# Transpositions woven between products, in a fused attention and FFN kernel

## The chip, the cores and the metric

The kernel runs on one core of a Trainium2 chip. The metric is the device time of one execution in microseconds (us); a profiled execution has a span from its first to its last instruction. Engines are named as in the profile: PE is TensorE's matrix products and PEld its weight loads, DVE is VectorE, ACT is ScalarE, POOL is GpSimd, SP is SyncE, which issues most transfers.

## The reference

Hashed attention over 4 batches of 8 heads (768 rows of 64), then a gated FFN over all 3072 tokens:

```
q_bits, k_bits = (q @ proj > 0), (k @ proj > 0)          # 6 bits: a bucket for each row
mask = q_bucket[:, None] == k_bucket[None, :]
scores = where(mask, (q @ k.T) / sqrt(64), -1e9)
attn = softmax(scores);  x = concat_heads(attn @ v)      # 3072 x 512
h = x @ w_in;  g = h * clip(h + 3, 0, 6) / 6;  out = g @ w_out   # 512 -> 2048 -> 512
```

## The kernel before

Work goes in 192 **steps** k, one for 128 query rows of a head (six steps a head, KT = 6). What one step does to the rows of its own number, and in which step it is emitted:

- `scores` (L305, L308; S below): four products of 384 columns into a PSUM pair `s`, emitted three steps ahead: step k emits S(k+3).
- `lowest` (L315): VectorE reads `s`, takes the row minimum and writes the tile `p`; step k emits `lowest(k+2)`. There are two `p` tiles, so p(k+2) takes the place of p(k).
- `exponential` (L327): ScalarE, in place on `p`; step k emits that of k+1.
- `transp` (L337; T below): six transpositions of 128 x 128 turn p(k) into two PSUM tiles `pt` (halves c = 0 and 1, three each).
- `split_p` (L360, L361): for each half ScalarE writes the high part `ph` and VectorE the rest `pl`.
- `values` (L374, L375; V below): for two steps' rows together, six products of 256 columns for each half, ph and pl in turn with v, into the PSUM tile `acc`. A half of the pair (k-2, k-1) is done in step k, the other in step k+1 (k even); from k = 102 on both in step k.
- `output` (L402): ScalarE copies `acc` to `y`.

Every sixth step holds a **hash** of the next head (`hash_qk`, L265 to L267: six products z, and `bits`, L276, on VectorE). The FFN of a chunk of 256 tokens is, for each of 16 slices, `gemm1` (L478 to L480, twelve products of 256 columns into `h`), `gate` on ScalarE and VectorE, and `gemm2` (L500 to L502, six products of 512 columns into `po`). The FFN of the first batch runs between steps 49 and 53; that of the others fills the steps from about 98 on, a `gemm1` and a `gemm2` of the slice before in each. `normalise` (rt, L436) transposes the softmax's divisors for it.

The order on TensorE, VectorE, ScalarE and GpSimd is that in which the program is written; every engine works through its own queue in order. `bank` hands out four PSUM banks in turn to pt, acc and h; `pair` hands out two bank pairs to s and z while no FFN runs (they alternate), and one alone once `ffn_on` is set. So while the FFN fills the steps, S(k+3) must wait until `lowest(k+2)` has read the pair.

In a step the main loop emits, before the change: T(k); `exponential(k+1)`; `lowest(k+2)`; V; the FFN's `gemm1`; S(k+3) (with the hash ahead of it); `split_p(k)`; `gemm2`.

Of the kernel before, what the change touches and what calls it, by code (L numbers as in the profile page):

```python
# [18 lines left out]
P = 128  # L19
NB = 6  # L20
ZK = 96
ZM = ZK + 2 * NB
# [18 lines left out]
def lsh_attention_moe(  # L41
# [10 lines left out]
    nc = tc.nc  # L52
# [3 lines left out]
    KT = S // P  # L56
    HW = S // 2
    QT = HW // P
    NCC = DM // P
    NFC = DF // P  # L60
# [3 lines left out]
    KM = D + 2 * NB  # L64
# [14 lines left out]
    def bank(shape, name: str, tag: str | None = None):  # L79

        nonlocal turn
        if tag is None:
            tag = ("pt", "pu")[turn % 2]
            turn += 1
        return ps.tile(shape, F32, name=name, tag=tag, bufs=2)
# [4 lines left out]
    def pair(name: str):  # L90

        nonlocal pair_turn
        pair_turn += 1
        tag = "s" if ffn_on or pair_turn % 2 else "po"
        return ps.tile([P, 2, 512], F32, name=name, tag=tag, bufs=1)


    thr = cp.tile([P, 1], F32, name="thr")
# [2 lines left out]
    ident = cp.tile([P, P], F32, name="ident")  # L101
# [3 lines left out]
    pjl = cp.tile([P, ZM], F32R, name="pjl")  # L105
# [3 lines left out]
    pjk, pjq = pjh[:, :ZM], pjh[:, ZK - D :]  # L109
# [97 lines left out]
    GB = HK + FB  # L207
# [22 lines left out]
    def scale_q(i: int):  # L230

        nc.gpsimd.tensor_scalar_mul(raws[i][:D], raws[i][:D], -SCALE)
# [27 lines left out]
    def hash_qk(i: int):  # L260
        k1, k2, q1, q2 = state[i]
        z = zs[i] = pair(f"z{i}")
        for j in range(2):
            c = slice(j * HW, (j + 1) * HW)
            nc.tensor.matmul(z[:ZM, j, :HW], lhsT=pjl[:], rhs=q1[:, c], start=True, stop=False)  # L265
            nc.tensor.matmul(z[:ZM, j, :HW], lhsT=pjk, rhs=k2[:, c], start=False, stop=False)
            nc.tensor.matmul(z[:ZM, j, :HW], lhsT=pjq, rhs=q2[:, c], start=False, stop=True)  # L267

    def bits(i: int):
        k1, k2, q1, q2 = state[i]  # L270
# [25 lines left out]
    scs, probs, outs = {}, {}, {}  # L296

    def scores(g: int):
        i, t = divmod(g, KT)
        k1, k2, q1, q2 = state[i]  # L300
        us = slice(t * P, (t + 1) * P)
        s = scs[g] = pair(f"s{g}")
        for c in range(2):
            cs_ = slice(c * HW, (c + 1) * HW)
            nc.tensor.matmul(s[:, c, :HW], lhsT=q1[:KM, us], rhs=k1[:KM, cs_], start=True, stop=False)  # L305
        for c in range(2):
            cs_ = slice(c * HW, (c + 1) * HW)
            nc.tensor.matmul(s[:, c, :HW], lhsT=q2[:, us], rhs=k2[:, cs_], start=False, stop=True)  # L308

    def lowest(g: int):  # L310

# [19 lines left out]
    pts, parts = {}, {}  # L331
    halves = 0

    def transp(g: int, c: int):
        pt = pts[g, c] = bank([P, QT, P], f"pt{g}_{c}")
        for x in range(QT):
            nc.tensor.transpose(pt[:, x], probs[g][0][:, c, x * P : (x + 1) * P], ident[:])  # L337
        if c:
            del probs[g]

    lent = []

# [23 lines left out]
    def values(u: int, c: int):  # L366
        vv = vvs[2 * u // KT]
        if c == 0:
            accs[u] = bank([P, 2 * P], f"acc{u}")
        acc = accs[u]  # L370
        hi, lo = parts.pop((u, c))
        for x in range(QT):
            kt = c * QT + x
            nc.tensor.matmul(acc[:], lhsT=vv[:, kt], rhs=hi[:, x], start=(kt == 0), stop=False)  # L374
            nc.tensor.matmul(acc[:], lhsT=vv[:, kt], rhs=lo[:, x], start=False, stop=(kt == KT - 1))  # L375

    adds = []

# [93 lines left out]
    def gemm1(n: str, fc: int, x, tag: str | None = None):  # L472
        hp = bank([P, TC], f"h{n}_{fc}", tag)
        wi = wt[2 * fc]
        for cc in range(NCC):
            xh, xl = x[cc]
            wc = slice(cc * P, (cc + 1) * P)
            nc.tensor.matmul(hp[:], lhsT=wi[:, 0, wc], rhs=xh, start=(cc == 0), stop=False)  # L478
            nc.tensor.matmul(hp[:], lhsT=wi[:, 0, wc], rhs=xl, start=False, stop=False)  # L479
            nc.tensor.matmul(hp[:], lhsT=wi[:, 1, wc], rhs=xh, start=False, stop=(cc == NCC - 1))  # L480
        return hp

    def gate(n: str, fc: int, hp, copy, engine, between=lambda: None):
# [12 lines left out]
    def gemm2(fc: int, po, gh, gl):  # L496
        wo = wt[2 * fc + 1]
        for u in range(TC // P):
            us = slice(u * P, (u + 1) * P)
            nc.tensor.matmul(po[u], lhsT=gh[:, us], rhs=wo[:, 0], start=(fc == 0), stop=False)  # L500
            nc.tensor.matmul(po[u], lhsT=gh[:, us], rhs=wo[:, 1], start=False, stop=False)  # L501
            nc.tensor.matmul(po[u], lhsT=gl[:, us], rhs=wo[:, 0], start=False, stop=(fc == NFC - 1))  # L502

    def store(b: int, t: int, po, end: bool = False):
        ob = sp.tile([P, TC // P, DM], F32, name=f"ob{b}_{t}", tag="ob")
# [283 lines left out]
    def lead(j: int):  # L789

        i, t = divmod(j, KT)
        n = i + 1
        alone = j < GF + LA
        if t == 0 and n < NJ:
            split_qk(n, nc.scalar.copy if ffn_on else nc.gpsimd.tensor_copy)
        if t in (1, 4):
            add()
        if t == 2:
            if i:
                split_v(i)  # L800

            if n + 1 < NJ and n != H + 1:
                get_qk(n + 1)
        if t == 3 and n < NJ:
            get_v(n)
            if alone:
                hash_qk(n)
        scores(j)
        if t == 3 and n < NJ and alone:
            bits(n)  # L810
        if t == 4 and n + 1 < NJ:
            scale_q(n + 1)
# [27 lines left out]
    with tc.manual_schedule(engines={ET.PE, ET.DVE, ET.Activation, ET.Pool}):  # L840
        split_qk(0, None)
        hash_qk(0)
        bits(0)
        scale_q(1)
        split_v(0)
        for x in range(3):
            ahead(0, x)
        for k in range(NS):
            end = GB if k < GB else NS
            i, t = divmod(k, KT)  # L850
            if k == HK - XE:
                lent += [cp.tile([P, 2 * WC], F32R, name=f"lent{n}", tag="w", bufs=NW) for n in range(2)]
            if k == GB:
                lent.clear()
            if k == HK:
                late["x"] = sp.tile([P, S], F32, name="late", tag="raw", bufs=1)
            for c in range(2):
                transp(k, c)
            if k + 1 < end:
                exponential(k + 1)  # L860
            if k + 2 < end:
                lowest(k + 2)
            if k == GB:
                next(first)
                pair_turn = 0

            third = k < GF + 2
            whole = False
            for _ in range(1 if third and k != HK else (2, 0)[k % 2]):
                if vnext < k - k % 2:  # L870
                    whole = value_half()
            if k >= GF - 2:
                next(fill, None)
            if whole and k >= GF:
                output(vnext // 2 - 1)
                whole = False

            hashed = k >= GF and (k + LA) % KT == 2
            if k >= GF and k + LA < end and not hashed:
                lead(k + LA)  # L880
            for c in range(2):
                split_p(k, c, third)
            if (k < GF or hashed) and k + LA < end:
                if hashed:
                    if (k + LA) // KT + 1 < NJ:
                        hash_qk((k + LA) // KT + 1)
                        bits((k + LA) // KT + 1)
                    next(fill, None)
                lead(k + LA)
            if whole:  # L890
                output(vnext // 2 - 1)
            if k >= GF - 2 and not hashed:
                next(fill, None)
            if k + LA >= NS:
                add()
            if HK - XE <= k < GB:
                for f in early_steps[k - HK + XE]:
                    f()

            if k < HK and t == 1 and i:  # L900
                with tc.issue_after(last.ins):
                    for n in range((i - 1) * WE // (H - 1), i * WE // (H - 1)):
                        load_w(n)
            if k == HK:
                late_x()
                with tc.issue_after(last.ins):
                    get_qk(H + 2)
                    for n in range(WE, WL):
                        load_w(n)
            if k + 1 == GB:  # L910
                first = first_ffn(lambda part: ahead(GB, part))
                next(first)
                for _ in range(2):
                    whole = value_half()
                output(vnext // 2 - 1)
                next(first)
        while vnext < NS:
            if value_half():
                output(vnext // 2 - 1)
        add()  # L920
        for _ in fill:
            pass
# [47 lines left out]
```

## Time and profile before

| | |
|---|---|
| median of 3 runs | 1042.86 us (1040.63 to 1043.05) |
| the profiled execution | 1040.82 us |
| its span | 1039.0 us |
| mean granted TensorE clock | 0.994 |
| PE busy / DVE busy | 97% / 66% of the span |
| L337 transpositions | 1152, 275 ns each as recorded, 162.2 us in all |

How rows read: "start us, us, engine line op out<-in xcount" in the views by time, where a row merges neighbours of one kind and a bracket gives the idle time before it and what ended it; recorded products overlap, so the distance between starts tells what one costs, and its duration does not. Rows of waits read "waiter <- releaser: us in total, times, longest us".

### The profile page before, as it was taken

To read this page: it belongs to the slowest core of one execution; us is meant where nothing else is said; L and a number is where in the kernel's file an instruction comes from. 1 tells how busy PE (TensorE), PEld (TensorE's weight loads), DVE (VectorE), ACT (ScalarE), POOL (GpSimd) and SP (SyncE) were. 2 spreads that over 40 slices of the span, in tenths; PEclk is the share of its full clock that TensorE was granted. 3 is DMA by queue.
4 is the path that set the end of the run, shared out by engine and by line. 5 is a ranking of instruction groups with operands and counts; after the bars stand their busy time and mean duration, and the time that the engine had idled before them with its cause. 6 is when DMAs were issued, how large, how long until landed. Compare 5 with 4: busy or idle time off the path is not lost.

```text
span 1039.0 us, 18911 instructions
## 1 busy us (share of the span) xinstructions
PE 1009.5 (97%) x6846; PEld 927.2 (89%) x6846; DVE 687.0 (66%) x1441; ACT 583.6 (56%) x1308; POOL 451.4 (43%) x439
## 2 busy tenths in 40 slices
PE   8999879999999999999999999999999999999998
PEld 7999868887989998899999999999899999899997
DVE  6999888999479998766656666655665563333332
ACT  6888855555478887645554555454455462333332
POOL 5677753334247775645444444544454232200100
PEclk9999989999999999999999999999999999999999
DMA  3666686000144555322222232222232011101000
GB/s 93 155 149 155 187 277 236 1 2 1 46 130 112 120 124 143 80 53 60 75 46 63 61 88 59 53 71 59 60 93 47 15 37 28 42 1 41 1 22 20
DMA packets 47380, 80.68 MB, mean 78 GB/s; under 512 B 5892, under 2 KB 27780, under 8 KB 47288
## 3 DMA queue, kind: packets, MB, share of 16 engines
q1 hardware_dynamic: 42808, 73.98, 24.2%
q0 software_dynamic: 4480, 5.51, 4.6%
q8 instruction: 54, 0.88, 0.4%
q14 instruction: 38, 0.31, 0.1%
HBM read 41.95 MB, written 18.09 MB: 58 GB/s over the span
## 4 chain that ended last, share of the span: by engine, by line
PE 83%; DVE 8%; issue 3%; POOL 2%; ACT 2%; DMA 1%; SPq 0%; DVEq 0%; POOLq 0%; ACTq 0%
PE pt L337 11%; PE h L479 7%; PE h L478 7%; PE h L480 7%; PE po L500 7%; PE po L502 7%; PE po L501 7%; PE acc L374 6%; PE acc L375 6%; PE s L305 6%; PE s L308 6%; DVE wr L175 1%; DVE pl L361 1%; DVE wr L177 1%; PE z L267 1%
## 5 line engine op out<-in xcount | busy, mean ns | idle before, releaser
L315 DVE TENSOR_SCALAR_CACHE_REDUCE p<-s 128x768 f32<-128x768 f32 x192 | 183.5, 956 | 103.5 <-PE pt L337 99.5
L361 DVE TENSOR_TENSOR pl<-pt,ph 128x384 fp32r<-128x384 f32 x376 | 191.8, 551 | 50.4 <-ACT ph L360 48.3
L360 ACT CAST ph<-pt 128x384 fp32r<-128x384 f32 x376 | 165.5, 480 | 57.4 <-PE pt L337 45.0
L327 ACT ACTIVATE p<-p,m 128x768 f32<-128x768 f32 x192 | 179.5, 935 | 5.1 <-DVE p L315 4.8
L487 ACT ACTIVATE g<-h,three 128x256 f32<-128x256 f32 x192 | 91.4, 476 | 155.9 <-PE h L480 141.6
L337 PE MATMUL pt<-ident,p 128*128 128x128 f32 x1152 | 162.2, 275 | 5.9 <-DVE pl L361 4.8
L493 POOL TENSOR_TENSOR gl<-g,gh 128x256 fp32r<-128x256 f32 x96 | 74.2, 773 | 203.7 <-DVE gh L492 160.0
L488 DVE SCALAR_TENSOR_TENSOR g<-g,h 128x256 f32<-128x256 f32 x192 | 80.6, 420 | 117.8 <-ACT g L487 115.3
L337 PEld LDWEIGHTS pt<-ident,p 128*128 128x128 f32 x1152 | 137.3, 141 | 23.6 <-PE pt L337 3.8
L374 PE MATMUL acc<-ph,vv 128*128 128x256 f32 x564 | 152.8, 303 | 1.0 <-DVE pl L361 1.0
L478 PE MATMUL h<-xh,w 128*128 128x256 f32 x512 | 147.7, 289 | 1.2 <-ACT y L402 1.2
L480 PE MATMUL h<-xh,w 128*128 128x256 f32 x512 | 143.4, 280 | 1.3 <-POOL w L196 1.3
L479 PE MATMUL h<-xl,w 128*128 128x256 f32 x512 | 143.2, 280 | 0.6 <-DVE xl L470 0.6
L375 PE MATMUL acc<-pl,vv 128*128 128x256 f32 x564 | 141.1, 283 | 0.0
L500 PE MATMUL po<-w,gh 128*128 128x512 f32 x320 | 126.7, 396 | 1.5 <-ACT gh L492 1.4
L501 PE MATMUL po<-w,gh 128*128 128x512 f32 x320 | 126.2, 394 | 0.9 <-POOL w L196 0.9
L502 PE MATMUL po<-w,gl 128*128 128x512 f32 x320 | 126.6, 396 | 0.0
L374 PEld LDWEIGHTS acc<-ph,vv 128*128 128x128 f32 x564 | 107.5, 191 | 2.2 <-DVE pl L361 1.9
L375 PEld LDWEIGHTS acc<-pl,vv 128*128 128x128 f32 x564 | 107.9, 191 | 0.0
L305 PE MATMUL s<-kk,qq 76*128 76x384 f32 x384 | 101.2, 344 | 2.5 <-ACT kk L281 1.5
L308 PE MATMUL s<-kk,qq 128*128 128x384 f32 x384 | 100.0, 341 | 0.0
L478 PEld LDWEIGHTS h<-xh,w 128*128 128x128 f32 x512 | 96.4, 188 | 3.8 <-ACT y L402 2.4
(134 smaller groups left out, 1999.5 us busy)
## 6 DMA issues: line engine op xcount, KB each, us to landing
raw<-in_qkT SPq DMA_DIRECT2D x32, 384.0 KB, 3.5
kk<-qq SPq DMA_DIRECT2D x62, 192.0 KB, 3.2
wr<-in_w_in SPq DMA_DIRECT2D x16, 512.0 KB, 7.1
wr<-in_w_out SPq DMA_DIRECT2D x16, 512.0 KB, 3.8
vr<-in_v SPq DMA_DIRECT2D x32, 192.0 KB, 2.4
qq<-qq SPq DMA_DIRECT2D x31, 192.0 KB, 3.6
out<-ob SPq DMA_DIRECT2D x11, 512.0 KB, 3.0
xr<-xs SPq DMA_DIRECT2D x9, 512.0 KB
```

Of the source, the lines that this page charges most:

```text
L315: nc.vector.tensor_scalar(out=pr_[:], in0=s[:, :, :HW], scalar1=CAP, scalar2=None, op0=ALU.min, op1=ALU.min, accum_out=m[:],)
L327: nc.scalar.activation(pr_[:], pr_[:], AF.Exp, bias=m[:], scale=-1.0, accum_out=sms[b][:, t, h : h + 1])
L337: nc.tensor.transpose(pt[:, x], probs[g][0][:, c, x * P : (x + 1) * P], ident[:])
L361: nc.vector.tensor_sub(lo[:, :, w], pt[:], hi[:, :, w].bitcast(F32))
L374: nc.tensor.matmul(acc[:], lhsT=vv[:, kt], rhs=hi[:, x], start=(kt == 0), stop=False)
L375: nc.tensor.matmul(acc[:], lhsT=vv[:, kt], rhs=lo[:, x], start=False, stop=(kt == KT - 1))
L478: nc.tensor.matmul(hp[:], lhsT=wi[:, 0, wc], rhs=xh, start=(cc == 0), stop=False)
L479: nc.tensor.matmul(hp[:], lhsT=wi[:, 0, wc], rhs=xl, start=False, stop=False)
L480: nc.tensor.matmul(hp[:], lhsT=wi[:, 1, wc], rhs=xh, start=False, stop=(cc == NCC - 1))
L500: nc.tensor.matmul(po[u], lhsT=gh[:, us], rhs=wo[:, 0], start=(fc == 0), stop=False)
L501: nc.tensor.matmul(po[u], lhsT=gh[:, us], rhs=wo[:, 1], start=False, stop=False)
L502: nc.tensor.matmul(po[u], lhsT=gl[:, us], rhs=wo[:, 0], start=False, stop=(fc == NFC - 1))
```

## The change

The six transpositions of a step are no longer emitted in one run. `transp` puts them on a list `woven`, and each product that is emitted through the new `mm` is followed by one of them, until the list is empty. Products of V, hash, S and FFN go through `mm`; the normalising transpositions do not. What is left is emitted by `flush` ahead of `split_p`, and in step GB = 52 at once.

```diff
+    woven = []
+
+    def mm(out: bass.AP, **kw):
+        nc.tensor.matmul(out, **kw)
+        if woven:
+            woven.pop(0)()
...
-    def transp(g: int, c: int):
-        pt = pts[g, c] = bank([P, QT, P], f"pt{g}_{c}")
-        for x in range(QT):
-            nc.tensor.transpose(pt[:, x], probs[g][0][:, c, x * P : (x + 1) * P], ident[:])
-        if c:
-            del probs[g]
+    def transp(g: int):
+
+        pr_, _ = probs.pop(g)
+
+        def one(x: int):
+            nc.tensor.transpose(
+                pts[g, x // QT][:, x % QT], pr_[:, x // QT, (x % QT) * P : (x % QT + 1) * P], ident[:]
+            )
+
+        for c in range(2):
+            pts[g, c] = bank([P, QT, P], f"pt{g}_{c}")
+        woven.extend(lambda x=x: one(x) for x in range(KT))
+
+    def flush():
+        while woven:
+            woven.pop(0)()
...
-            nc.tensor.matmul(acc[:], lhsT=vv[:, kt], rhs=hi[:, x], start=(kt == 0), stop=False)
-            nc.tensor.matmul(acc[:], lhsT=vv[:, kt], rhs=lo[:, x], start=False, stop=(kt == KT - 1))
+            mm(acc[:], lhsT=vv[:, kt], rhs=hi[:, x], start=(kt == 0), stop=False)
+            mm(acc[:], lhsT=vv[:, kt], rhs=lo[:, x], start=False, stop=(kt == KT - 1))
...
-            for c in range(2):
-                transp(k, c)
+            transp(k)
+            if k == GB:
+                flush()
...
             if k >= GF and k + LA < end and not hashed:
                 lead(k + LA)
+            flush()
             for c in range(2):
                 split_p(k, c, third)
```

(In `hash_qk`, `scores`, `gemm1` and `gemm2` the products change to `mm` in the same way.)

TensorE in the even step 36, before the change: scores, the run of six, then the six products of V(36), whose first carries the wait on VectorE. In the names, pt36_0 is half 0 of step 36, and ph17_0 and pl17_0 hold half 0 of the pair 34 and 35.

```order
L305 MATMUL s38_1449<-kk_6_1161,qq_6_1162 128x384 x2
L308 MATMUL s38_1449<-kk_6_1161,qq_6_1162 128x384 x2
L337 MATMUL pt36_0_1456<-ident_69,p36_1399 128x128 [waits DVE_49,Activation_49]
L337 MATMUL pt36_0_1456<-ident_69,p36_1399 128x128 x2
L337 MATMUL pt36_1_1460<-ident_69,p36_1399 128x128 [waits Activation_49]
L337 MATMUL pt36_1_1460<-ident_69,p36_1399 128x128 x2
L374 MATMUL acc17_1468<-ph17_0_1408,vv5_1231 128x256 [waits DVE_49,PE_49]
L375 MATMUL acc17_1468<-pl17_0_1409,vv5_1231 128x256
```

The same place after it (L100 is `mm`, L346 the transposition):

```order
L100 MATMUL s38_1449<-kk_6_1161,qq_6_1162 128x384 x4
L100 MATMUL acc17_1462<-ph17_0_1408,vv5_1231 128x256 [waits DVE_49,Activation_49]
L346 MATMUL pt36_0_1456<-ident_69,p36_1393 128x128 [waits DVE_49,PE_49]
L100 MATMUL acc17_1462<-pl17_0_1409,vv5_1231 128x256
L346 MATMUL pt36_0_1456<-ident_69,p36_1393 128x128
L100 MATMUL acc17_1462<-ph17_0_1408,vv5_1231 128x256
L346 MATMUL pt36_0_1456<-ident_69,p36_1393 128x128
L100 MATMUL acc17_1462<-pl17_0_1409,vv5_1231 128x256
L346 MATMUL pt36_1_1457<-ident_69,p36_1393 128x128 [waits Activation_49]
```

V(36) moved directly behind the scores, and the second wait on VectorE, now on the first transposition, is that for pl17_0 of step 35, which the product behind it reads.

TensorE in the odd step 121, in the part with the FFN, before: the run, then the first of twelve `gemm1` products (h1_0_15), behind which S(124) stands.

```order
L337 MATMUL pt121_0_6605<-ident_69,p121_6481 128x128 [waits Activation_49]
L337 MATMUL pt121_0_6605<-ident_69,p121_6481 128x128 x2
L337 MATMUL pt121_1_6609<-ident_69,p121_6481 128x128 [waits DVE_49]
L337 MATMUL pt121_1_6609<-ident_69,p121_6481 128x128 x2
L478 MATMUL h1_0_15_6617<-xh1_0_5665,w30_3392 128x256
```

The same place after it, from the step's first product to its last transposition:

```order
L100 MATMUL h1_0_15_6611<-xh1_0_5665,w30_3392 128x256 [waits Activation_49]
L346 MATMUL pt121_0_6605<-ident_69,p121_6475 128x128 [waits DVE_49,PE_49]
L100 MATMUL h1_0_15_6611<-xl1_0_5666,w30_3392 128x256
L346 MATMUL pt121_0_6605<-ident_69,p121_6475 128x128
L100 MATMUL h1_0_15_6611<-xh1_0_5665,w30_3392 128x256
L346 MATMUL pt121_0_6605<-ident_69,p121_6475 128x128
L100 MATMUL h1_0_15_6611<-xh1_0_5665,w30_3392 128x256
L346 MATMUL pt121_1_6606<-ident_69,p121_6475 128x128 [waits DVE_49]
L100 MATMUL h1_0_15_6611<-xl1_0_5666,w30_3392 128x256
L346 MATMUL pt121_1_6606<-ident_69,p121_6475 128x128
L100 MATMUL h1_0_15_6611<-xh1_0_5665,w30_3392 128x256
L346 MATMUL pt121_1_6606<-ident_69,p121_6475 128x128
```

The last transposition moved behind six of the twelve products; the other six and S(124) still follow it. On VectorE, ScalarE and GpSimd the order is the same before and after.

More of the change, by code (lines that the diff above doesn't have):

```diff
@@ L264, in hash_qk @@
             c = slice(j * HW, (j + 1) * HW)
-            nc.tensor.matmul(z[:ZM, j, :HW], lhsT=pjl[:], rhs=q1[:, c], start=True, stop=False)
-            nc.tensor.matmul(z[:ZM, j, :HW], lhsT=pjk, rhs=k2[:, c], start=False, stop=False)
-            nc.tensor.matmul(z[:ZM, j, :HW], lhsT=pjq, rhs=q2[:, c], start=False, stop=True)
+            mm(z[:ZM, j, :HW], lhsT=pjl[:], rhs=q1[:, c], start=True, stop=False)
+            mm(z[:ZM, j, :HW], lhsT=pjk, rhs=k2[:, c], start=False, stop=False)
+            mm(z[:ZM, j, :HW], lhsT=pjq, rhs=q2[:, c], start=False, stop=True)
     def bits(i: int):
@@ L304, in scores @@
             cs_ = slice(c * HW, (c + 1) * HW)
-            nc.tensor.matmul(s[:, c, :HW], lhsT=q1[:KM, us], rhs=k1[:KM, cs_], start=True, stop=False)
+            mm(s[:, c, :HW], lhsT=q1[:KM, us], rhs=k1[:KM, cs_], start=True, stop=False)
         for c in range(2):
             cs_ = slice(c * HW, (c + 1) * HW)
-            nc.tensor.matmul(s[:, c, :HW], lhsT=q2[:, us], rhs=k2[:, cs_], start=False, stop=True)
+            mm(s[:, c, :HW], lhsT=q2[:, us], rhs=k2[:, cs_], start=False, stop=True)
     def lowest(g: int):
@@ L477, in gemm1 @@
             wc = slice(cc * P, (cc + 1) * P)
-            nc.tensor.matmul(hp[:], lhsT=wi[:, 0, wc], rhs=xh, start=(cc == 0), stop=False)
-            nc.tensor.matmul(hp[:], lhsT=wi[:, 0, wc], rhs=xl, start=False, stop=False)
-            nc.tensor.matmul(hp[:], lhsT=wi[:, 1, wc], rhs=xh, start=False, stop=(cc == NCC - 1))
+            mm(hp[:], lhsT=wi[:, 0, wc], rhs=xh, start=(cc == 0), stop=False)
+            mm(hp[:], lhsT=wi[:, 0, wc], rhs=xl, start=False, stop=False)
+            mm(hp[:], lhsT=wi[:, 1, wc], rhs=xh, start=False, stop=(cc == NCC - 1))
         return hp
@@ L499, in gemm2 @@
             us = slice(u * P, (u + 1) * P)
-            nc.tensor.matmul(po[u], lhsT=gh[:, us], rhs=wo[:, 0], start=(fc == 0), stop=False)
-            nc.tensor.matmul(po[u], lhsT=gh[:, us], rhs=wo[:, 1], start=False, stop=False)
-            nc.tensor.matmul(po[u], lhsT=gl[:, us], rhs=wo[:, 0], start=False, stop=(fc == NFC - 1))
+            mm(po[u], lhsT=gh[:, us], rhs=wo[:, 0], start=(fc == 0), stop=False)
+            mm(po[u], lhsT=gh[:, us], rhs=wo[:, 1], start=False, stop=False)
+            mm(po[u], lhsT=gl[:, us], rhs=wo[:, 0], start=False, stop=(fc == NFC - 1))
     def store(b: int, t: int, po, end: bool = False):
```

## The prediction

> **What bounds the kernel now.** I read the page first, then busy time by stretch, then the waits of each engine, then the instructions of a few steps in order of time. In the page, TensorE is busy 97% of the span, and the chain that ended last is TensorE for 83% of it.
>
> ```profile
> span 1039.0 us, 18911 instructions
> PE 1009.5 (97%) x6846; PEld 927.2 (89%) x6846; DVE 687.0 (66%) x1441; ACT 583.6 (56%) x1308; POOL 451.4 (43%) x439
> PE 83%; DVE 8%; issue 3%; POOL 2%; ACT 2%; DMA 1%; SPq 0%; DVEq 0%; POOLq 0%; ACTq 0%
> L361 DVE TENSOR_TENSOR pl<-pt,ph 128x384 fp32r<-128x384 f32 x376 | 191.8, 551 | 50.4 <-ACT ph L360 48.3
> ```
>
> Busy time in three stretches that hold nearly all steps (columns: PE, PEld, DVE, ACT, POOL, then clock, DMA and GB/s) shows two regimes, both with a dense TensorE at full clock:
>
> ```profile
> 24.84:111.00 86.16, 86.16 (x645) 83.71 (x644) 79.23 (x159) 75.13 (x172) 62.59 (x51) 1.00 0.65 163
> 299.63:407.05 107.42, 106.05 (x785) 102.06 (x785) 98.98 (x198) 91.94 (x210) 72.68 (x59) 1.00 0.51 123
> 430.41:862.30 431.89, 430.24 (x2972) 399.11 (x2971) 263.33 (x562) 220.26 (x504) 190.59 (x205) 1.00 0.24 58
> ```
>
> The first two are the *bare* steps (k = 4 to 42, 54 to 100: transpositions T, six value products V, scores S); VectorE is 92% busy beside TensorE there. The third is the *FFN* steps. So a TensorE wait added in any of them lengthens the time. The waits of VectorE name who follows the transpositions:
>
> ```profile
> DVE p L315 <- PE pt L337: 99.5, 141, 2.2
> ```
>
> `lowest(k+2)` takes one of two p tiles and cannot start before T(k) has read it: 141 of its 192 starts are released by a transposition. The end of T(k), not its sum, is therefore what the change moves.
>
> **The price of a transposition on TensorE.** One bare step, and the next one's start:
>
> ```profile
> 91.00 0.87 PE L337 MATMUL pt<-ident,p 128*128 128x128 f32 x6
> 92.43 0.52 PE L305 MATMUL s<-kk,qq 76*128 76x384 f32 x2
> 93.15 0.82 PE L337 MATMUL pt<-ident,p 128*128 128x128 f32 x6
> 93.72 0.36 PE L374 MATMUL acc<-ph,vv 128*128 128x256 f32 x1
> 93.92 0.29 PE L375 MATMUL acc<-pl,vv 128*128 128x256 f32 x1
> 94.05 0.28 PE L374 MATMUL acc<-ph,vv 128*128 128x256 f32 x1
> 95.22 0.88 PE L337 MATMUL pt<-ident,p 128*128 128x128 f32 x6
> ```
>
> Products of 256 columns follow each other every 0.12 us. The second product starts 0.77 after the first transposition; less its own predecessor's 0.12, six transpositions cost 0.65, or 0.11 each, the last one (with a product behind it) like the others. No row shows a lone transposition between two products. Upper bound: 0.11, what the last of a run already costs. Lower bounds: 0.057, half of what 256 further columns cost (0.23 against 0.12 in the FFN rows below), if the weight load behind it were hidden; and 0.03, the distance at which the record lets the first product start behind the last transposition (93.15 + 5 x 0.109 = 93.69 to 93.72). I take 0.11, the nearest row: a transposition followed by a product. Then TensorE's own sum does not change: the weave saves nothing.
> The Trainium skill, "TensorE: Matmul & The Clock Gate", section "Step-by-step: what each phase is for", says the queue pulls weight loads ahead, so that the next tile's weights load while this one's matmul runs. Read for this change, a transposition behind a product would cost its stream alone, and the sum would be that of the second rival. The trace bears it out only one instruction deep: 0.12 us products hide their loads, and a transposition's 0.11 is not its stream.
>
> **Bare steps, even k: the cover goes.** VectorE around the same steps:
>
> ```profile
> 91.91 0.96 DVE L315 TENSOR_SCALAR_CACHE_REDUCE p<-s 128x768 f32<-128x768 f32 x1 [0.24 <-PE pt L337]
> 92.79 1.02 DVE L361 TENSOR_TENSOR pl<-pt,ph 128x384 fp32r<-128x384 f32 x2
> 94.00 0.96 DVE L315 TENSOR_SCALAR_CACHE_REDUCE p<-s 128x768 f32<-128x768 f32 x1 [0.20 <-PE pt L337]
> 391.10 1.02 DVE L361 TENSOR_TENSOR pl<-pt,ph 128x384 fp32r<-128x384 f32 x2
> 392.26 0.52 PE L337 MATMUL pt<-ident,p 128*128 128x128 f32 x3 [0.32 <-DVE pl L361]
> ```
>
> T(33), begun at 91.00, ends at 91.87; `lowest(35)` starts 0.04 later; pl of step 33, half 0, starts 0.88 after that and takes 0.55. The last two rows give pl's end to TensorE: 0.14, say 0.15. So from the end of T(j), odd j, to a TensorE instruction that needs pl(j,0): 0.04 + 0.88 + 0.55 + 0.15 = 1.62.
> V of the even step j+1 is that instruction (its second product reads pl; the order has the wait on the first transposition). Before, V(j), S (0.72) and T(j+1) stood between: V(34) starts at 93.72, 1.85 after T(33)'s end, without a wait. Now V(j) is woven into T(j) and T(j+1) stands behind V's first product: only S and that product cover the 1.62, and the transpositions queue behind the wait. Their run is then 5 x (0.11 + 0.12) = 1.15 from first to last start plus 0.27 (one recorded duration): T(j) end to T(j+1) end is 1.62 + 1.15 + 0.27 = 3.04.
> Odd k: the fourth transposition takes the bank that pl(k-1,0) frees, the same 1.62 after the end of T(k-1) (without waits it would come at 1.37). Then 2 x 0.23 + 0.27: 2.35. Where the hash's z products (1.05, rows below) stand between, they cover the wait, and the step is dense: 0.11 - 0.27 + 1.05 + 0.72 + 0.12 + 1.15 + 0.27 = 3.15.
> A head has three pairs: 2 x (3.04 + 2.35) + 3.04 + 3.15 = 16.97 us. Before, from T(31) to T(37) (and, in the last two rows, the first z of a hash and the S behind its six):
>
> ```profile
> 86.84 0.49 PE L337 MATMUL pt<-ident,p 128*128 128x128 f32 x3
> 100.47 0.49 PE L337 MATMUL pt<-ident,p 128*128 128x128 f32 x3
> 398.19 0.33 PE L265 MATMUL z<-qq,pjl 128*108 128x384 f32 x1
> 399.24 0.52 PE L305 MATMUL s<-kk,qq 76*128 76x384 f32 x2
> ```
>
> 13.63 us. +3.34 per head. The stretches hold 38 and 46 steps, 14 heads: +46.8. In each batch's last head the transpositions already wait on VectorE (the 0.32 above); I take off 2. ScalarE is no second link: per pair two exponentials, four ph and one y are about 4.4 of 5.4 us, and they follow chains that end earlier.
>
> **FFN steps, odd k: S waits.** T(121), the twelve h products, S(124); and S(125) of the even step behind:
>
> ```profile
> 503.63 0.39 PE L502 MATMUL po<-w,gl 128*128 128x512 f32 x1
> 503.86 0.82 PE L337 MATMUL pt<-ident,p 128*128 128x128 f32 x6
> 504.63 0.28 PE L479 MATMUL h<-xl,w 128*128 128x256 f32 x1
> 504.75 0.28 PE L480 MATMUL h<-xh,w 128*128 128x256 f32 x1
> 505.91 0.52 PE L305 MATMUL s<-kk,qq 76*128 76x384 f32 x2
> 504.71 0.96 DVE L315 TENSOR_SCALAR_CACHE_REDUCE p<-s 128x768 f32<-128x768 f32 x1 [1.44 <-PE pt L337]
> 505.60 0.08 DVE L315 DVE_READ_ACCUMULATOR p<-s 128x1 f32 x1
> 509.77 0.08 DVE L315 DVE_READ_ACCUMULATOR p<-s 128x1 f32 x1
> 511.52 0.52 PE L305 MATMUL s<-kk,qq 76*128 76x384 f32 x2
> 17.25 0.08 DVE L315 DVE_READ_ACCUMULATOR p<-s 128x1 f32 x1
> 17.39 0.61 PE L305 MATMUL s<-kk,qq 76*128 76x384 f32 x2
> ```
>
> With the FFN on, scores have one bank pair: S(k+3) needs `lowest(k+2)`. At 505.68 it is done, S is due at 505.91: 0.23 of slack, and the shortest distance seen is 0.06 (17.33 to 17.39). Woven, the last transposition starts behind six h products; six remain, so S is due 0.11 + 0.70 = 0.81 after that start, but ready only at 0.27 + 0.04 + 0.97 + 0.06 = 1.34. Stall 0.53, per odd step; what is queued behind S (the second FFN product, the next T) moves with it. In the even step the slack is 1.67, the delay 0.70: nothing, and pl(k-1) of the odd step is done over 1 us before V. The slack of 0.23 recurs in 35 odd steps (the first S and the last below; in those with a hash z takes S's place, on the same bank), and three more have 0.60:
>
> ```profile
> 443.06 0.08 DVE L315 DVE_READ_ACCUMULATOR p<-s 128x1 f32 x1
> 443.38 0.52 PE L305 MATMUL s<-kk,qq 76*128 76x384 f32 x2
> 845.50 0.08 DVE L315 DVE_READ_ACCUMULATOR p<-s 128x1 f32 x1
> 845.81 0.52 PE L305 MATMUL s<-kk,qq 76*128 76x384 f32 x2
> ```
>
> 35 x 0.53 + 3 x 0.16 = 19.
>
> **The rest.** Steps 2 and 44 to 50 (five even ones, where TensorE already waits often): bounded by 0 and 5 x 0.93; I take 3. Slots before h look 0.005 longer than within a run (504.63 - 503.86 = 0.77, less 0.117, over six): five slots in some 40 odd steps, 1. VectorE, ScalarE and GpSimd keep their order. SyncE's queue has some loads of q, k and v one or two places earlier, ahead of stores of y and of the hash bits' copies; they serve the next head, microseconds later: 0.
> Sum: 46.8 - 2 + 19 + 3 + 1 = 68 us. The profiled execution took 1040.8 (span 1039.0), so 1109; its time lies 2 under the median of the three runs, so I say 1110.
>
> **Rivals.**
> Slower still: the odd bare steps without a hash get the even ones' full chain (their first transposition also waits a pl, though an older one). 28 steps x (3.04 - 2.35) = 19: 1129. Against it: that pl is two steps old.
> The transposition costs 0.057 woven. A bare head becomes 2 x (2.77 + 2.24) + 2.77 + 2.84 = 15.63, +2.0, 28 in all; 91 later steps save 6 x 0.052, 28; S's stall becomes 0.58, +20. Sum +20: 1061. Against it: 0.11 for the last of each run. The skill's rule above speaks for it. Near it, at 1062, lies the case that VectorE's chain costs little in the bare steps and the FFN stall alone stays.
> Only the bare steps pay (S's stall hidden, if `lowest` starts earlier than its order allows it now): 1110 - 19 = 1091.
> Not slower: one mechanism, the slot behind a woven transposition is the recorded 0.03. Then a bare head is 14.9 (+1.3, 18 in all), later steps save 91 x 6 x 0.08 = 44, S stalls 35 x 0.61 = 21: 1035, faster. Between 0.03 and 0.057 the sum passes zero near 0.035; above that the change loses. Against it: the same rows let the second product wait until 0.2 after the first.
> That the change doesn't weave can be set aside: in the order 1116 of 1152 transpositions stand alone behind another operation.
>
> **Chances.** Both waits as costed, 0.68, own range 1094 to 1124. Slower still 0.10. Bare steps alone 0.07. 0.057 or FFN alone 0.10. Not slower 0.05, of which 0.04 faster. The range 1060 to 1130 holds all but the last and the edges. 0.3% of the time, 3 us, is what a measurement can tell from no change: faster 0.04, same 0.01, slower 0.95.
>
> **What would show it.** In the profile after: TensorE idle before pt in bare even steps, released by pl, about 0.9 each and some 45 of them; `lowest` still 0.04 behind the last transposition; S in odd FFN steps idle 0.5, released by p; transpositions 0.11 after each other's product. The bare stretches some 45 us longer, the FFN one 19. Wrong if the products behind transpositions come closer than 0.2 in pairs, or if the even waits stay under 0.3.

## The result, and the profile after

The woven kernel takes 1130.36 us (median of 4 runs, 1129.21 to 1135.09) against 1042.78 of the kernel before: a ratio of 1.085, 95% interval 1.082 to 1.089. It is slower, for the most part by the mechanism that the prediction gave, and by more than it gave: 88 us in place of 68, 0.4 us beyond the upper end of the range.

The page of the kernel after: span, busy time of each engine, the granted clock in tenths, and the group of instructions whose wait grew most.

```profile
span 1127.9 us, 18861 instructions
PE 1037.5 (92%) x6846; PEld 938.1 (83%) x6846; DVE 677.3 (60%) x1441; ACT 598.1 (53%) x1308; POOL 450.1 (40%) x439
PEclk9999999999999999999999999999999999999999
L322 DVE TENSOR_SCALAR_CACHE_REDUCE p<-s 128x768 f32<-128x768 f32 x192 | 183.7, 957 | 241.8 <-PE pt L346 239.8
```

TensorE has the same 6846 products at the same clock, and is now idle for 90 us of the span in place of 30. (Its recorded busy time is 28 us larger for the same products: one that no longer overlaps its predecessor adds its whole recorded duration.) The waits of TensorE, all steps, and that of VectorE for the transpositions:

```profile
PE pt L346 <- DVE pl L378: 45.4, 53, 2.9
PE s L100 <- DVE p L322: 9.9, 28, 0.4
PE z L100 <- DVE p L322: 4.6, 13, 0.4
PE rt L453 <- POOL rb L443: 3.7, 6, 0.8
DVE p L322 <- PE pt L346: 239.8, 182, 2.3
```

The first row is mainly the even bare step (43 of the 53 waits, 34.8 of the 45.4 us, lie in the bare stretches 4 to 42 and 54 to 100), the next two the odd FFN step, as predicted. 182 of 192 starts of `lowest` are now released by a transposition, against 141. The fourth row is one that the prediction did not name. Its total was 3.8 us before the change too, but elsewhere: in steps 107 to 191 it was 0.3 and is 3.4 now.

Where the time went, from the end of a step's sixth transposition (counted in the two traces, six to a step), before and after:

| stretch | before | after | longer by | predicted |
|---|---|---|---|---|
| bare steps 4 to 42 | 25.65 to 111.82 | 27.50 to 138.12 | 24.5 | 44.8 for both bare stretches |
| steps 42 to 54 | to 300.51 | to 329.64 | 2.8 | 3 with the start and 100 to 107 |
| bare steps 54 to 100 | to 407.87 | to 464.61 | 27.6 | (above) |
| steps 100 to 107 | to 431.23 | to 492.02 | 4.1 | (above) |
| FFN steps 107 to 191 | to 862.67 | to 952.22 | 28.8 | 20 |

With 1.9 up to step 4 the sum, before rounding, is 89.6; the two profiled times, 1129.7 and 1040.8, are 88.9 apart, since what stands behind step 191 is 0.7 shorter.

A bare step in order of time, TensorE and then VectorE (the idle time before a row stands in its bracket):

```profile
117.25 0.27 PE L346 MATMUL pt<-ident,p 128*128 128x128 f32 x1
117.27 0.95 PE L100 MATMUL s<-kk,qq 76*128 76x384 f32 x4
118.06 0.28 PE L100 MATMUL acc<-ph,vv 128*128 128x256 f32 x1
119.14 0.30 PE L346 MATMUL pt<-ident,p 128*128 128x128 f32 x1 [0.80 <-DVE pl L378]
119.19 0.37 PE L100 MATMUL acc<-pl,vv 128*128 128x256 f32 x1
119.40 0.27 PE L346 MATMUL pt<-ident,p 128*128 128x128 f32 x1
119.42 0.36 PE L100 MATMUL acc<-ph,vv 128*128 128x256 f32 x1
120.32 0.27 PE L346 MATMUL pt<-ident,p 128*128 128x128 f32 x1
121.31 0.33 PE L100 MATMUL z<-qq,pjh 128*108 128x384 f32 x1
121.65 0.80 PE L100 MATMUL s<-kk,qq 76*128 76x384 f32 x3
117.55 0.96 DVE L322 TENSOR_SCALAR_CACHE_REDUCE p<-s 128x768 f32<-128x768 f32 x1 [0.48 <-PE pt L346]
118.44 1.02 DVE L378 TENSOR_TENSOR pl<-pt,ph 128x384 fp32r<-128x384 f32 x2
121.51 0.08 DVE L322 DVE_READ_ACCUMULATOR p<-s 128x1 f32 x1
```

T(35) ends at 117.52; `lowest` starts 0.03 later; pl 0.89 after that; the first transposition of T(36) starts at 119.14, which is 1.62 after the end of T(35). From there the last one starts 1.18 later, and T(36) ends at 120.59: a step of 3.07, predicted 3.04. A transposition and the product behind it take 0.23 together (119.40 to 119.63 in full order), as much as the two cost apart.

An odd FFN step, from the last transposition to the scores and the product behind them:

```profile
570.37 0.27 PE L346 MATMUL pt<-ident,p 128*128 128x128 f32 x1
571.07 0.28 PE L100 MATMUL h<-xh,w 128*128 128x256 f32 x1
571.70 0.96 PE L100 MATMUL s<-kk,qq 76*128 76x384 f32 x4 [0.36 <-DVE p L322]
572.50 0.62 PE L100 MATMUL po<-w,gh 128*128 128x512 f32 x2
570.68 0.96 DVE L322 TENSOR_SCALAR_CACHE_REDUCE p<-s 128x768 f32<-128x768 f32 x1 [2.17 <-PE pt L346]
571.57 0.08 DVE L322 DVE_READ_ACCUMULATOR p<-s 128x1 f32 x1
```

`lowest` is done at 571.65, the scores start 0.05 later. The bracket's 0.36 counts from the recorded end of the last h product (571.35); it was due 0.12 after that product's start, so the wait is 0.51. Then the FFN products come 0.80 after the scores' start (571.70 to 572.50), which is 0.1 more than without a wait, as a table below shows.

### The profile page after: what moved, and what is told of

It is laid out like the page before. It is cut to its first block, busy times and chain, and to the rows that moved or that the text cites. A ratio compares the mean times of both kernels' runs of the same rounds, so it can differ in the third digit from the quotient of the medians.

```text
span 1127.9 us, 18861 instructions
## 1 busy us (share of the span) xinstructions
PE 1037.5 (92%) x6846; PEld 938.1 (83%) x6846; DVE 677.3 (60%) x1441; ACT 598.1 (53%) x1308; POOL 450.1 (40%) x439
## 4 chain that ended last, share of the span: by engine, by line
PE 51%; DVE 3%; issue 1%; POOL 1%; DMA 0%; ACT 0%; DVEq 0%; POOLq 0%; ACTq 0%
PE po L100 17%; PE h L100 15%; PE s L100 6%; PE acc L100 5%; PE pt L346 5%; DVE p L322 3%; PE z L100 2%; PE rt L453 1%; DMA xs<-y 0%; POOL rb L443 0%; ACT y L419 0%; POOL xs L398 0%; DVE ob L530 0%; POOL gl L510 0%; ACT ob L529 0%
## 5 line engine op out<-in xcount | busy, mean ns | idle before, releaser
L346 PE MATMUL pt<-ident,p 128*128 128x128 f32 x1152 | 276.7, 276 | 48.8 <-DVE pl L378 45.4
L100 PE MATMUL h<-xh,w 128*128 128x256 f32 x1024 | 223.7, 296 | 2.5 <-POOL w L203 1.3
L346 PEld LDWEIGHTS pt<-ident,p 128*128 128x128 f32 x1152 | 160.6, 140 | 68.6 <-issue 54.9
L100 PE MATMUL po<-w,gh 128*128 128x512 f32 x640 | 201.2, 395 | 2.4 <-ACT gh L509 1.4
L100 PE MATMUL s<-kk,qq 76*128 76x384 f32 (+1 forms) x768 | 181.0, 357 | 12.6 <-DVE p L322 9.9
L100 PE MATMUL acc<-pl,vv 128*128 128x256 f32 x564 | 191.5, 347 | 0.0
L100 PE MATMUL acc<-ph,vv 128*128 128x256 f32 x564 | 183.8, 333 | 2.5 <-DVE lent L378 1.2
L100 PEld LDWEIGHTS h<-xh,w 128*128 128x128 f32 x1024 | 171.6, 188 | 7.2 <-ACT y L419 2.4
L100 PE MATMUL h<-xl,w 128*128 128x256 f32 x512 | 150.4, 294 | 0.6 <-DVE xl L487 0.6
L100 PEld LDWEIGHTS s<-kk,qq 76*128 76x128 f32 (+1 forms) x768 | 127.3, 190 | 28.1 <-DVE p L322 21.2
L100 PEld LDWEIGHTS po<-w,gh 128*128 128x128 f32 x640 | 113.6, 187 | 17.8 <-ACT gh L509 2.5
L100 PE MATMUL po<-w,gl 128*128 128x512 f32 x320 | 126.2, 394 | 0.0
L100 PEld LDWEIGHTS acc<-ph,vv 128*128 128x128 f32 x564 | 108.4, 192 | 4.7 <-ACT ph L377 2.2
L100 PEld LDWEIGHTS acc<-pl,vv 128*128 128x128 f32 x564 | 109.5, 194 | 0.0
L419 ACT COPY y<-acc 128x256 f32<-128x256 f32 x84 | 31.6, 376 | 136.4 <-PE acc L100 136.4
```

The costliest lines, as they stand in the source:

```text
L100: nc.tensor.matmul(out, **kw)
L346: nc.tensor.transpose(pts[g, x // QT][:, x % QT], pr_[:, x // QT, (x % QT) * P : (x % QT + 1) * P], ident[:])
L419: nc.scalar.copy(y, acc[:])
```

## The experiments

**The run moved, not woven.** The transpositions stay together and are emitted behind the sixth product.

```diff
         if woven:
-            woven.pop(0)()
+            behind += 1
+            if behind == KT:
+                flush()
```

> The six transpositions stay together in one run, which stands behind the sixth of the products that followed it before (flushed there; nothing is woven). Theory (the place of the last transposition and the cover in front of it decide, not the weave itself): the last transposition stands where the weave puts it, so the time is the woven kernel's 1130 us less at most 3 (in odd bare steps the fourth transposition comes later and no longer waits), 1125 to 1132. Rival (the change of instruction at each slot costs TensorE time of its own): a run has none of it, 1043 to 1070.

1120.5 us, ratio 1.076 (1.074 to 1.079). The place, not the weave, carries nearly all of it: the FFN steps 107 to 191 lose 27.2 us, where the woven kernel loses 28.8, with no transposition between two products. It is 4.5 below the expected range: the odd bare steps are dense again, 2.14 as before the change, where the woven kernel has 2.39 (medians, from one step's last transposition to the next one's); 28 such steps make 7.0 of the 7.5 that the bare stretches got back. The expectation had allowed at most 3 for this.

**One part at a time.** The weave in steps below 102 alone, in steps from 102 on alone, and in the even steps from 102 on alone:

```diff
-            if k == GB:
+            if k == GB or not (k < GF + 2):                   # the early steps
+            if k == GB or not (k >= GF + 2):                  # the FFN steps
+            if k == GB or not (k >= GF + 2 and k % 2 == 0):   # even FFN steps
                 flush()
```

> The weave in steps k below 102 alone; behind them the run of six as before the change. Theory: what the trace of the woven kernel has lost by step 100, 56.1 us, and part of the next steps' 4.1: 1043 + 56 to 60 = 1099 to 1103. Rival (the parts are not independent: with the early steps late, the FFN steps gain or lose something too): outside of 1095 to 1107.

> The weave in steps k from 102 on alone. Theory: 28.8 us of the FFN steps and up to 3 of the steps 102 to 107: 1043 + 29 to 32 = 1072 to 1075; in the odd steps the scores wait 0.64 us a pair as in the woven kernel. Rival (what the FFN steps lose depends on the bare steps' delay): 1060 or less, or 1085 or more.

> The weave in the 45 even steps from 102 on alone, where the scores have 1.67 us of slack. Theory (a transposition costs 0.11 between products as in a run; nothing waits): the time before, 1043, within 2. Rival (a product in front hides a transposition's weight load, 0.05 each): 45 x 6 x 0.05 = 14 less, 1029. Second rival (each change of instruction costs more than 0.11): over 1048.

1096.1, 1074.6 and 1041.95 us, beside 1040.84 of the kernel before on that chip. 55.2 and 33.8 more add up to 89.0; the whole weave costs 88: the two parts are independent. The first lies 3 below its expected range: 2 of them because the kernel before takes 1040.84 there and not 1043, and steps 100 to 107 are 1.4 shorter, not longer. The third is the price of a woven transposition: 270 of them moved behind products change the time by a factor of 1.001 (1.000 to 1.002). Neither 14 us less nor 5 more: it costs what it costs in a run. Two woven transpositions in such a step, and the weight load of the product between them:

```profile
507.39 0.27 PE L346 MATMUL pt<-ident,p 128*128 128x128 f32 x1
507.62 0.27 PE L346 MATMUL pt<-ident,p 128*128 128x128 f32 x1
507.39 0.19 PEld L100 LDWEIGHTS acc<-pl,vv 128*128 128x128 f32 x1
```

A transposition and a product take 0.23 together, the 0.11 of a transposition in a run and the 0.12 of a product. The Trainium skill, "TensorE: Matmul & The Clock Gate", section "Step-by-step: what each phase is for", says that the queue pulls weight loads ahead, under the matmul that runs. The trace agrees, since the load of the product behind starts with the transposition, at 507.39. What fails is the prediction's reading of it, that the transposition would then cost its stream alone.

**Even and odd bare steps apart.**

```diff
-            if k == GB:
+            if k == GB or k >= GF + 2 or not (k % 2 == 0):   # even steps woven
+            if k == GB or k >= GF + 2 or not (k % 2):        # odd steps woven
                 flush()
```

> The weave in the even steps below 102 alone; T of the odd steps is a run again. Theory (the even step loses its cover): from the end of T(j), j odd, V(j) and S take 0.72 each, so the first woven transposition, ready at 1.62, waits little; but T(j+1) ends at 3.04 as in the woven kernel, since V and T are spread over each other, and the next odd run, whose fourth transposition takes the bank that pl(j+1,0) frees 1.62 after that, ends 2.1 behind it: a pair takes 5.15 against 4.21, 45 pairs x 0.94 = 42, 1083 (1073 to 1090). Rival (each woven step costs the same): half of the 55 that the weave in all steps below 102 cost, 1068.

> The weave in the odd steps below 102 alone; T of the even steps is a run again. Theory: from the end of T(j), j odd, S and the run of T(j+1) cover 1.38 of the 1.62 that pl needs, V(j+1) waits 0.24, and nothing else is late: 45 pairs x 0.24 = 11, 1052 (1045 to 1058). Rival (each woven step costs the same): 1068. With the run before it the two do not add up to 55, if the waits overlap: by the theory 53, by the rival 55.

1085.2 us with the even steps woven (45.0 more, 42 expected): the even steps take 3.08, so they lose their cover whatever the odd ones do, and the odd ones are dense at 2.14. 1062.4 us with the odd steps woven: 22.1 more, where 11 was expected and 28 was the rival's. The two add up to 67, not to the 53 or 55 of the expectation; how the waits overlap when both are woven was not tried. Of TensorE around the even step's run there, and its waits:

```profile
113.52 0.27 PE L346 MATMUL pt<-ident,p 128*128 128x128 f32 x1
114.35 0.83 PE L346 MATMUL pt<-ident,p 128*128 128x128 f32 x6
115.41 0.36 PE L100 MATMUL acc<-ph,vv 128*128 128x256 f32 x1 [0.23 <-DVE pl L378]
115.61 0.28 PE L100 MATMUL acc<-pl,vv 128*128 128x256 f32 x1
115.73 0.28 PE L100 MATMUL acc<-ph,vv 128*128 128x256 f32 x1
PE acc L100 <- DVE pl L378: 11.7, 43, 0.4
```

T(j) ends at 113.79, and the first value product starts 1.62 later: the chain is the one costed. What was costed wrongly is when the product is due. Without a wait it is recorded 0.57 behind the start of such a run (93.15 to 93.72 in the prediction's rows, and in 38 of the 42 even bare steps there), here 1.06 behind it. So it was due at 114.92, 1.13 after T(j)'s end and not 1.38, the wait is 0.49, and 45 pairs make 22. The bracket's 0.23 counts from the recorded end of the last transposition. The 0.20 to the product behind is no part of it: it is the same behind every such run, with a wait or without.

**Three p tiles.** `lowest(k+2)` then waits only for its scores. The room comes from v, with one pair of tiles, loaded and split two steps later; the same in the kernel before is the control.

```diff
-        pr_ = sp.tile([P, 2, HW], F32, name=f"p{g}", tag="p", bufs=2)
+        pr_ = sp.tile([P, 2, HW], F32, name=f"p{g}", tag="p", bufs=3)
...
-        vv = vvs[i] = sp.tile([P, KT, P], F32R, name=f"vv{i}", tag="vv")
+        vv = vvs[i] = sp.tile([P, KT, P], F32R, name=f"vv{i}", tag="vv", bufs=1)
...
+        if t == (3 if i == H else 4) and i:
+            split_v(i)
+        if t == 5 and n < NJ:
+            get_v(n)
```

> The woven kernel with three p tiles in place of two, so that lowest(k+2) no longer takes the tile that T(k) reads; to make room v has one pair of tiles in place of two, and its load and split stand two steps later. Theory (the late last transposition costs time only through lowest, which waits for it): in the FFN steps lowest is done long before S, 38 pairs x 0.64 = 24 back; in the bare steps pl of half 0 is no longer behind lowest, ends about 0.8 after the last transposition in place of 1.62, and is covered by S and one product (0.83) again: most of the 56 back. 1045 to 1060. Rival (the woven slots or the pt banks themselves hold TensorE, whatever lowest does): over 1110. Between them, about 1106: the FFN part alone comes back, since VectorE still does lowest ahead of pl.

> The same three p tiles and one pair of v tiles in the kernel before the change, as a control. Theory (TensorE is dense there, and what VectorE waits for lies beside it): 1041 within 4. Rival (the third tile shortens any kernel, or the one pair of v tiles holds TensorE): 10 or more off.

1070.25 us woven, 1048.48 not woven: with three tiles the weave costs 21.8 us in place of 88. The woven kernel with three tiles, VectorE and then TensorE in a bare step, and the waits of TensorE; in the last row, that of the control:

```profile
102.72 0.95 DVE L322 TENSOR_SCALAR_CACHE_REDUCE p<-s 128x768 f32<-128x768 f32 x1
103.81 1.07 DVE L378 TENSOR_TENSOR pl<-pt,ph 128x384 fp32r<-128x384 f32 x2
103.50 0.27 PE L346 MATMUL pt<-ident,p 128*128 128x128 f32 x1
105.36 0.28 PE L100 MATMUL acc<-ph,vv 128*128 128x256 f32 x1
105.48 0.27 PE L346 MATMUL pt<-ident,p 128*128 128x128 f32 x1
PE acc L100 <- POOL vv L299: 19.1, 16, 2.5
PE rt L453 <- POOL rb L443: 5.5, 6, 2.1
PE pt L346 <- DVE pl L378: 5.2, 6, 2.9
PE acc L374 <- POOL vv L292: 8.8, 15, 2.3
```

`lowest` now starts 0.78 ahead of the step's last transposition, and pl follows that at once. The 53 waits of pt for pl are 6, as many as before the change, the waits of s and z for p are gone from the list; woven bare steps are 2.09 even and 2.09 odd, and the scores of an odd FFN step start 0.81 after the last transposition's start, the distance that the prediction had worked out for them without the wait. So the mechanism stands: the late last transposition costs time through `lowest`, and the woven slots cost next to nothing. The Trainium skill, "Perfetto Trace Analysis", section "Identifying Performance Opportunities", says that a gap which repeats for a stretch can mean that there is no room for the next tile; the 53 waits that one more tile turns into 6 agree. The 10 us over 1060 are of the size of the experiment's own cost: v in one pair of tiles makes TensorE wait 19.1 us, and even the control 8.8, which fits the control's being 7.6 slower than its original and not within 4. Of the 21.8, 10.5 are lost in the bare stretches, where these waits are 14.7 in place of the control's 5.4, and 5.2 in steps 107 to 191, 3.5 of them at the five ends of chunks, which the next experiment but one is about. The other 6 lie at the edges and were not tried apart.

**pl ahead of lowest**, in the woven bare steps, on VectorE:

```diff
-            if k + 2 < end:
+            if k + 2 < end and not plain:        # plain: the bare steps
                 lowest(k + 2)
...
                 split_p(k, c, third)
+            if k + 2 < end and plain:
+                lowest(k + 2)
```

> The woven kernel, with lowest(k+2) emitted behind split_p(k) in the bare steps, so that VectorE writes pl ahead of it. Theory (the bare steps wait for pl because lowest stands in front of it): pl of half 0 ends about 0.8 after the last transposition in place of 1.62, the even steps' wait of 0.9 goes and the odd ones' 0.25: 40 to 52 of 56 back, 1078 to 1090; lowest ends about 2.5 after T(k), the exponential 3.7, T(k+2) is due 4.2 after. Rival (the wait is for the pt bank or in TensorE's own slots): 1120 or more; second rival (the exponential is now late): T waits for p on ScalarE, and less than half comes back.

1192.9 us: not 40 back but 63 more. ScalarE and VectorE there:

```profile
137.70 0.84 ACT L377 CAST ph<-pt 128x384 fp32r<-128x384 f32 x2
138.19 1.02 DVE L378 TENSOR_TENSOR pl<-pt,ph 128x384 fp32r<-128x384 f32 x2 [1.52 <-ACT ph L377]
139.13 0.95 DVE L322 TENSOR_SCALAR_CACHE_REDUCE p<-s 128x768 f32<-128x768 f32 x1
140.12 0.94 ACT L334 ACTIVATE p<-p,m 128x768 f32<-128x768 f32 x1 [1.58 <-DVE p L322]
141.06 0.84 ACT L377 CAST ph<-pt 128x384 fp32r<-128x384 f32 x2
```

On ScalarE `exponential(k+1)` stands ahead of ph(k). With `lowest` behind pl, the exponential waits for `lowest`, ph for the exponential, pl for ph, and `lowest` for pl: a circle of 3.36 us a step (137.70 to 141.06). The expectation traced the exponential to the transpositions and not to what is queued behind it on its own engine. The run says nothing against the chain through pl, and nothing for it.

**The run back between the normalising pairs.**

```diff
     def normalise(name: str, x, rb, tag: str | None = None):
         rt = bank([P, TC], f"rt{name}", tag)
+        flush()
```

> The woven kernel, with what is left of the list emitted ahead of each normalising pair rt, so that in the five odd steps at the end of a chunk the six transpositions stand between two such pairs again. Theory (the run covered the way rt, xr on VectorE, rb on GpSimd, rt): those steps took 7.59 against 6.54 before; 5 x 1.05 = 5 back, 1123 to 1128. Rival (those steps are long for the scores' wait, as the others): within 1 of 1130.

1121.98 us, ratio 1.078 (1.076 to 1.081): 8 less, more than the 5 expected, and 1 below the expected range. The end of a chunk before the change (first three rows), after it (two), and the wait in the FFN steps with this edit:

```profile
492.20 0.38 PE L436 MATMUL rt<-ident,rb 128*128 128x128 f32 x2
492.42 0.82 PE L337 MATMUL pt<-ident,p 128*128 128x128 f32 x6
493.39 0.33 PE L436 MATMUL rt<-ident,rb 128*128 128x128 f32 x1 [0.15 <-POOL rb L426]
556.12 0.38 PE L453 MATMUL rt<-ident,rb 128*128 128x128 f32 x2
557.31 0.44 PE L453 MATMUL rt<-ident,rb 128*128 128x128 f32 x2 [0.81 <-POOL rb L443]
PE rt L454 <- POOL rb L443: 0.3, 2, 0.2
```

Before, the run stood between two normalising pairs, and beside it VectorE multiplied with the first and GpSimd, in the one `rb` tile, wrote for the second. That way takes 1.19 from pair to pair, woven or not. Woven, the run stands behind both pairs, and of the 1.19 TensorE is idle for 0.81 in place of 0.15. With the edit steps 107 to 191 lose 22.3 in place of 28.8, and 102 to 107, where such pairs stand too, 3.1 less. Of the 6.5, the waits of rt are 3.1 (3.4 before the edit, 0.3 with it). The rest fits the scores or z of the same five steps: woven, they start 0.06 behind `lowest`, as in the other odd steps, and with the edit 0.61 or 0.82 behind it, so that they no longer wait. The rival was right that these steps wait there too.

**How far behind.** From step 102 on the run stays together, behind the first or the third product (with the edit above; below 102 nothing is changed):

```diff
-            woven.pop(0)()
+            behind += 1
+            if behind == 3:      # 1 in the other
+                flush()
```

> In the steps from 102 on the six transpositions stay one run, emitted behind the first product that followed them before (and ahead of each normalising pair); below 102 nothing is changed. Theory (in the odd steps the scores have 0.17 to spare): the last transposition is 0.12 later, nothing waits: 1041 to 1045. Rival (each product put ahead of the run costs its 0.12): 38 x 0.12 = 5 and the edge, 1046 or more.

> The same with the run behind the third product. Theory: the last transposition is 0.35 later, 0.18 more than there is to spare, and since the weight load of the scores carries the wait, its 0.11 is added: 38 x 0.29 = 11, 1052 to 1056. Rival (the wait alone counts, its load is hidden): 38 x 0.18 = 7, 1046 to 1050. Second rival (any place behind a product costs the whole 0.64): 1065.

1042.2 us (1.002, 1.001 to 1.003) and 1050.06 us (1.010, 1.008 to 1.011). In steps 110 to 185, odd and without a hash, read off the starts in the traces (us, the commonest value):

| the last transposition is | last transposition's start to scores | p done to scores | first score to second |
|---|---|---|---|
| in the run before (22 of 25 steps) | 1.51 | 0.23 | 0.18 |
| behind one product (21) | 1.40 | 0.13 | 0.21 |
| behind three (22) | 1.33 | 0.06 | 0.28 |
| woven, behind six (25) | 1.33 | 0.06 | 0.28 |
| woven, three p tiles (25) | 0.81 to 0.83 | over 1.4 | 0.18 |

The first product spends slack and costs 0.02 to 0.03 a pair; from the third on the distance stands at its floor of 1.33, and what is moved further is waited. Beside the wait the second score comes 0.10 later: three products cost 0.17 of wait and 0.10, and the pair is 0.26 longer (4.43 against 4.17 in its even half), six cost 0.64 (4.81). The 0.29 of the expectation is nearly met in the step. Its total, 1052 to 1056, is missed by 2, and 1050.06 lies at the edge of the first rival's range, 1046 to 1050. The change is 9.8 from the 1040.24 that the kernel before takes on that chip, where the expectation had 11 and this rival 7: only some 33 pairs in steps 107 to 191 lose the 0.26, and the pairs at the ends of chunks lose nothing. So the step decides for the theory; the total alone would not.

## Why the prediction fell short, point by point

- **TensorE dense, so that an added wait lengthens the time; the end of T(k) moves it through `lowest`:** right. Three p tiles cut that link and three quarters of the loss go.
- **A woven transposition costs 0.11:** right. Even FFN steps woven change next to nothing; the second rival (0.057) and the one that ends faster (0.03) both rest on a price that is not there.
- **Even bare steps, 1.62 and 3.04:** right to 0.03, and again 1.62 where only odd steps are woven.
- **Odd bare steps, 2.35:** 2.39. The fear of the rival "slower still" (3.04 there) did not come; its time, 1129, was met for other reasons.
- **Bare heads, +3.34 each:** mis-sized; a head takes 2 x (3.07 + 2.39) + 3.41 + 3.19 = 17.5 in place of 16.97, and the bare stretches 52.1 more in place of 44.8. The step that failed is "where the hash's z products stand between, they cover the wait, and the step is dense": that step is 3.41, not 3.15, and the even one behind it 3.19, not 3.04. z takes one of the two bank pairs, so the S behind it needs `lowest` of the latest scores: that is done at 121.59 in the rows above, and S starts at 121.65, 0.34 behind the last z, where 0.18 is the rule; with three p tiles, where `lowest` is early, the step is 3.12. The prediction had looked for a wait of the scores for `lowest` in the FFN steps alone. In the even step behind it pl starts 1.00 after `lowest` in place of the 0.88 that the prediction took for every step; that is so in all 14 heads, before the change too, but there it cost nothing.
- **FFN odd steps, 35 x 0.53 and 3 x 0.16:** the mechanism right, the term mis-sized: 0.64 each, 22.3 in all in place of 19. The second score comes 0.10 later behind one that waited than it does without a wait. The three steps at 0.16 were wrong too: they stand at ends of chunks and wait like the others, 0.06 behind `lowest`.
- **Normalising transpositions:** no term at all. The change's part named them as untouched; that the run *covered* the way from one pair to the next was not looked for. Giving the run its place back returned 6.5 of the FFN steps' 28.8, about half of it waits of rt, and 3.1 between 102 and 107.
- **Edges, 3, and slots, 1:** the edges cost 8.7: 1.9 up to step 4, 2.8 in steps 42 to 54, 4.1 in 100 to 107. The last is largely the same normalising pairs; the first two were seen in the traces alone and not tried apart. Slots longer by 0.005 are within what the even FFN steps leave open: 1.1 us (0.2 to 2.1) for 270 woven transpositions, 0.004 each.

Added up, the misses are 7.3 in the bare steps, 8.8 in the FFN steps and 5.7 at the edges. All have one sign. Each of those whose cause was found is something that the run, or a place further back in the queue, had hidden for nothing: a bank's release, a weight load, the way between two normalising pairs.

## What to carry to other kernels

Before moving a run of instructions on a full in-order engine, list what it covers in each place where it stands, not only in the common step: here it covered the way to pl, the way to the scores' bank, and the way from one normalising pair to the next. Then ask who waits for its last instruction, and compare that slack with the delay: the scores had 0.17 us to spare, one product in front was nearly free, three were not. Weaving pays nothing where an instruction costs the same between others as in a run; a third tile that lets the waiting reader go ahead is what takes the last instruction off the path.

## What the runs showed of the hardware

A wait of the scores cost TensorE more than the wait: in all 25 woven steps and in 22 with the run behind three products, the second score started 0.28 behind the first, where 0.18 is the distance without a wait. The weight loads show where the 0.10 comes from, before the change and after it:

```profile
505.80 0.30 PEld L305 LDWEIGHTS s<-kk,qq 76*128 76x128 f32 x2
571.70 0.64 PEld L100 LDWEIGHTS s<-kk,qq 76*128 76x128 f32 x4 [0.55 <-DVE p L322]
```

Before, the load of the first score's weights starts 0.11 ahead of the score (505.80 and 505.91), under the product in front. Woven, the load itself waits for `lowest` and starts with the score (571.70), so nothing hides it. That this is the whole of the 0.10 is inferred. The value products of the run with odd steps woven show no such addition: the second comes 0.20 behind the first with the wait and without it.
